# Two 64-byte buffers move in front of the three large tiles of a one-core decode kernel

## The chip, the core and the metric

The kernel runs on one core of a Trainium2 chip. Its time is the time on the device in microseconds (us), as the runs give it. The profile adds one profiled execution, with the start and duration of each instruction on TensorE (PE, with weight loads apart as PEld), VectorE (DVE), ScalarE (ACT), GpSimd (POOL) and SyncE (SP), and with the transfers between the chip's memory and the core's on-chip memory (SBUF). SBUF has 128 partitions; a buffer takes the same byte range in each of them, so that one byte address per buffer says where it lies.

## The reference

One decode step of a transformer block, batch B = 2, one new token each, model width D = 512, in bf16:

- q = layernorm(x) @ wq, in 32 heads of Dh = 128. For each of the 2 x 32 heads, with its own cache of Sk = 8192 keys and values: scores = q . k / sqrt(128), p = softmax(scores), o = p @ v. The heads' outputs side by side, times wo, are added to x and give h.
- gate = layernorm(h) @ W_gate, up = layernorm(h) @ W_up (512 to 1376), gate times (gate > 0), times up, times W_down (1376 to 512), added to h.

The two caches have 2 x 32 x 8192 x 128 bf16 values each, 134 MB per cache. All of it is read once, so the kernel moves some 281 MB into SBUF. There is one multiplication and one addition per cached value, since every head has a single query.

## The kernel before

**Tiles.** A "quad" is four heads of one batch row. Its keys are 8 MB: one tile of 128 partitions x 32768 bf16, 65,536 bytes per partition (`TILE`, L54). The three buffers `bufs[0..2]` of that size (`tile0`, `tile1`, `tile2`, made in L90 from the pool `big`) hold all that streams in. There are 16 quads; the first 15 are whole steps (`steps[0..14]`, `LASTQ` is 14), and the last quad is worked as two pairs of heads (`steps[15]`, `steps[16]`) whose keys and values come in pieces of 4 MB or 1 MB. The step's key tile and value tile go round the three buffers (L137, L138: buffers 2i mod 3 and 2i+1 mod 3). wq lies in the first half of `tile2` before the first steps; at the end wo, W_gate, W_up and W_down take freed halves of the three tiles (L121 to L127).

**A transfer.** `load_tile` (L160) issues a transfer on SyncE's queue: each partition's row is one contiguous run of 65,536 bytes in memory and one in SBUF. The rows of W_gate and W_up (L613 to L616) are 5,504 bytes, those of W_down and of the last wo pieces 1,024 to 8,192.

**A step.** For step i: PE transposes 24 or 32 of the tile's 256 key columns and multiplies them with q (`scores_pe`, L329, with copies by ACT, L353); DVE multiplies all other keys by the q of their head (`products`, L378, in place, with `qrep`) and adds the products up by halving four times and a reduction (`scores`, L396, L398); DVE and ACT make the maximum and the exponentials (`largest_of_own`, L411; L418 writes the sums of the exponentials into `zs`); DVE lays them out as weights (`place_own`, L423, into `pgq`); PE multiplies the weights with the value tile in 64 matrix products (`values`, L449). Every fourth step or so the group of heads is normalised (`close`, L318, where `own_sums`, L299, reads `zs`).

**Order.** The order on each engine is written out by hand (`tc.manual_schedule`, L187); nothing reorders it. The value tile of step i+1 is loaded into the buffer of step i's keys as soon as DVE has reduced them (L528, SyncE waits for L398); the key tile of step i+2 goes into the buffer of step i's values when PE has used them (L552, SyncE waits for L449). So two transfers are under way or queued while one step is computed. Both wait on SyncE's queue, in this order.

**Where things lie.** Pools are laid out in the order in which they are made (L80 to L83), and buffers in the order of their lines, each rounded up to 32 bytes. A reserved block fills the bytes up to 16,384, four constants take 128 bytes, and then `front` begins: `qTs` (L87) and `ocol` (L88), 128 bytes each. The tiles follow. In the built program `tile0` begins at byte 16,768 of each partition, `tile1` at 82,304 and `tile2` at 147,840, each 384 bytes behind a multiple of 512, and 128 behind a multiple of 256. Behind the tiles stand the pool `consts` (`qrep` and all below it, among them `zs`, 64 bytes, L99, and `qzp`, 64 bytes, L103) and the pool `small`. `qzp` holds the queries of the last two heads' pairs, and PE loads it as weights in the last two steps (L342).

Of the kernel before, what the change touches and what calls it, by code (L numbers as in the profile page):

```python
# [23 lines left out]
def kernel(  # L24
# [14 lines left out]
    P = nc.NUM_PARTITIONS  # L39
    B, Sq, D = A_x.shape  # L40
# [6 lines left out]
    bf16 = mybir.dt.bfloat16  # L47
    f32 = mybir.dt.float32
# [3 lines left out]
    NQ = Hq // NH  # L52
# [27 lines left out]
    front = ctx.enter_context(tc.tile_pool(name="front", bufs=1))  # L80
    big = ctx.enter_context(tc.tile_pool(name="big", bufs=1))
    consts = ctx.enter_context(tc.tile_pool(name="consts", bufs=1))
# [3 lines left out]

    qTs = front.tile([P, B, Hq], bf16)  # L87
    ocol = front.tile([P, Hq, B], bf16)  # L88

    bufs = [big.tile([P, TILE], bf16, name=f"tile{k}") for k in range(3)]  # L90

# [4 lines left out]
    pv = consts.tile([P, VG * Dh], f32)  # L96
    pick = consts.tile([P, VG, 4, NH], f32)
    zc = consts.tile([P, B, NQ, NH], f32)
    zs = consts.tile([P, B, NQ], f32)  # L99
    own = consts.tile([P, NH], f32)  # L100
    ownb = consts.tile([P, NH, VG], bf16)
    ecol = consts.tile([P, TILE // Dh], bf16)
    qzp = consts.tile([P, 2, 16], bf16)  # L103
    qz = consts.tile([P, 2 * QZ], bf16)
    ident = consts.tile([P, P], bf16)
    ident_f = consts.tile([QZ, QZ], f32)
# [647 lines left out]
```

## Time and profile before

| | us |
|---|---|
| median of 3 runs | 662.56 (661.42 to 663.75) |
| the profiled execution's own time | 661.14 |
| its span, from the first to the last instruction | 659.3 |
| DVE busy | 557.4 (85%) |
| PE busy (matmuls) | 353.1 (54%) |
| ACT busy | 122.9 (19%) |
| transfers: share of the span in which the 16 DMA engines carry packets of SyncE's queue | 99.0% |

The page gives the DMA engines' share as a mean over 16 engines. A packet is a contiguous run that one of them moves; the packets under 512 bytes are almost all the 4-byte notes that tell a semaphore of a transfer's end. In the answers by stretch ("DMA share, GB/s"), a packet's bytes and time can fall into the neighbouring stretch, so that a share can stand a little above 1.00; the quotient of the two columns is the rate of a busy DMA engine, times 16. "issue to landing" is the time from the instruction that starts a transfer until its semaphore says that it has ended, waiting in the queue included. PEclk is the granted TensorE clock as a share of full speed; its mean is 0.759 here.

### The profile page before, as it was taken

The page shows a single profiled execution, that of the slowest core. Times are in us where ns is not written, and L with a number is a line of the kernel's source. Part 1 is how long each engine was busy: PE and PEld are TensorE (multiplying, and loading weights), DVE is VectorE, ACT ScalarE, POOL GpSimd, SP SyncE. Part 2 cuts the span into 40 slices and gives each one's busy share as a digit, 9 for nine tenths or more (in the row PEclk, how much of TensorE's full clock was granted, in tenths as well). Part 3 has the DMA queues.
Part 4 walks back from the last instruction along what each step waited for, and adds up shares of the span by engine and source line. Part 5 has one row for each costly group of instructions (what it writes and reads, how often), then busy time and mean ns, then how long its engine had stood idle before and what let it go on. Part 6 is the DMA issues. An engine that isn't in the chain of part 4 may idle for free.

```text
span 659.3 us, 5118 instructions
## 1 busy us (share of the span) xinstructions
PE 353.1 (54%) x2123; PEld 160.8 (24%) x2123; DVE 557.4 (85%) x248; ACT 122.9 (19%) x335; POOL 7.6 (1%) x35
## 2 busy tenths in 40 slices
PE   3540924709174480917438092562909358291987
PEld 1220311304022130402214041220403224030456
DVE  2399697989979699997979979896997969999981
ACT  1130030301103020020302102030210304201870
POOL 3000000000000000000000000000000000000010
PEclk9865875959778595977859687695968869686985
DMA  9999999999999999999999999999999999999997
GB/s 382 445 442 445 433 399 441 441 446 434 414 433 430 441 438 421 433 437 426 441 425 434 437 426 433 421 442 437 425 434 427 437 438 425 437 430 412 426 414 279
DMA packets 7946, 281.40 MB, mean 427 GB/s; under 512 B 882, under 2 KB 1780, under 8 KB 2804
## 3 DMA queue, kind: packets, MB, share of 16 engines
q1 hardware_dynamic: 7920, 281.09, 99.0%
q8 instruction: 16, 0.26, 0.2%
q14 instruction: 6, 0.05, 0.0%
q10 hardware_dynamic: 4, 0.00, 0.0%
HBM read 281.09 MB, written 0.00 MB: 426 GB/s over the span
## 4 chain that ended last, share of the span: by engine, by line
DVE 47%; DMA 34%; PE 17%; ACT 1%; issue 1%; SPq 0%; DVEq 0%; ACTq 0%
DMA tile<-in_A_k_cache_dram 28%; DVE tile L378 21%; DVE tile L396 20%; PE pv_ps L449 16%; DMA tile<-in_A_v_cache_dram 3%; DVE scol L398 3%; DMA tile<-in_B_W_up_dram 2%; DVE pgq L423 1%; DMA tile<-in_B_W_down_dram 1%; ACT ecol L418 1%; DVE pm L402 1%; DVE qrep L398 0%; DVE pm L413 0%; DVE hmax L415 0%; PE z_ps L308 0%
## 5 line engine op out<-in xcount | busy, mean ns | idle before, releaser
L449 PE MATMUL pv_ps<-tile,pgq 128*16 128x512 bf16 x960 | 241.8, 417 | 236.4 <-DVE pgq L423 225.0
L378 DVE TENSOR_TENSOR tile<-tile,qrep 128x29696 bf16<-128x29696 bf16 (+3 forms) x16 | 232.4, 14522 | 37.7 <-DMA tile<-in_A_k_cache_dram 37.7
L396 DVE TENSOR_TENSOR tile<-tile 128x14848 bf16<-128x14848 bf16 (+7 forms) x68 | 236.5, 3477 | 2.3
L449 PEld LDWEIGHTS <-pgq 128*16 128x16 bf16 x960 | 91.0, 97 | 376.4 <-DVE pgq L423 235.1
L353 ACT ACTIVATE tile<-t_ps 128x1024 bf16<-128x1024 bf16 x53 | 52.5, 1022 | 18.6 <-PE t_ps L352 18.2
L454 ACT ACTIVATE pv<-pv_ps 16x512 f32<-16x512 f32 (+1 forms) x16 | 9.4, 589 | 234.0 <-PE pv_ps L449 233.9
L418 ACT ACTIVATE ecol<-scol,nmax 128x256 bf16<-128x256 f32 x14 | 7.1, 508 | 196.7 <-DVE nmax L417 196.7
L352 PE MATMUL t_ps<-ident,tile 128*128 128x128 bf16 x424 | 32.7, 230 | 18.1 <-DMA tile<-in_A_k_cache_dram 18.1
L343 PE MATMUL row_ps<-tile,qz 128*24 128x512 bf16 (+1 forms) x98 | 31.0, 399 | 18.6 <-ACT tile L353 18.5
L352 PEld LDWEIGHTS <-tile 128*128 128x128 bf16 x424 | 26.1, 103 | 33.3 <-DMA tile<-in_A_k_cache_dram 18.7
L398 DVE TENSOR_REDUCE scol<-tile 128x232 f32<-128x1856 bf16 (+1 forms) x14 | 28.9, 2067 | 0.5
L423 DVE TENSOR_TENSOR pgq<-ecol,ownb 128x1024 bf16<-128x1024 bf16 x15 | 10.4, 692 | 10.3 <-ACT ecol L418 10.3
L384 ACT ACTIVATE tile<-tile 128x128 bf16<-128x128 bf16 x60 | 17.6, 295 | 1.9 <-DVE tile L378 1.9
L378 DVE TENSOR_TENSOR tile<-tile,qpair 128x4096 bf16<-128x4096 bf16 (+3 forms) x4 | 15.5, 3882 | 0.0
L343 PEld LDWEIGHTS <-qz 128*24 128x24 bf16 (+1 forms) x98 | 7.9, 93 | 28.7 <-issue 23.5
L249 PE MATMUL q_ps<-tile,xn 128*2 128x512 bf16 x32 | 9.7, 469 | 8.4 <-DMA tile<-in_A_wq_dram 8.4
L252 DVE CAST tile<-q_ps 2x512 bf16<-2x512 f32 x8 | 5.4, 678 | 10.2 <-PE q_ps L249 10.2
L370 ACT ACTIVATE scol<-sc_ps 32x24 f32<-32x24 f32 (+1 forms) x56 | 11.7, 209 | 7.7 <-PE sc_ps L365 7.2
L365 PE MATMUL sc_ps<-ident_f,tile 24*128 24x24 f32 (+2 forms) x68 | 7.2, 220 | 11.0 <-ACT tile L361 11.0
L361 ACT ACTIVATE tile<-row_ps 24x512 f32<-24x512 f32 (+2 forms) x17 | 10.0, 586 | 13.4 <-PE row_ps L343 13.4
L312 DVE RECIPROCAL rz<-z_ps 128x16 f32<-128x16 f32 (+1 forms) x4 | 0.9, 236 | 13.1 <-PE z_ps L308 13.1
L384 ACT ACTIVATION_READ_ACCUMULATOR tile<-tile 128x1 f32 x60 | 11.3, 188 | 0.0
(130 smaller groups left out, 132.9 us busy)
## 6 DMA issues: line engine op xcount, KB each, us to landing
tile<-in_A_k_cache_dram SPq DMA_DIRECT2D x2, 4096.0 KB, 22.8
tile<-in_A_wq_dram SPq DMA_DIRECT2D x1, 4096.0 KB, 12.1
tile<-in_A_v_cache_dram SPq DMA_DIRECT2D x1, 4096.0 KB, 19.7
tile<-in_A_v_cache_dram SPq DMA_DIRECT2D x4, 1024.0 KB, 21.0
tile<-in_A_wo_dram SPq DMA_DIRECT2D x1, 2048.0 KB, 24.2
tile<-in_B_W_gate_dram SPq DMA_DIRECT2D x2, 688.0 KB, 13.8
tile<-in_B_W_up_dram SPq DMA_DIRECT2D x2, 688.0 KB, 12.9
tile<-in_A_wo_dram SPq DMA_DIRECT2D x1, 1024.0 KB
```

The source lines that it names most:

```text
L343: nc.tensor.matmul(out=row_ps, lhsT=z, rhs=s.kt[:, (nv + c0 + k) * Dh:(nv + c0 + k + 4) * Dh], start=(u == 0), stop=(u == U - 1),)
L352: nc.tensor.transpose(t_ps[:, k, :], s.kt[:, t * Dh:(t + 1) * Dh], ident)
L353: nc.scalar.activation(out=s.kt[:, (nv + c0) * Dh:(nv + c0 + TPC) * Dh], in_=t_ps.rearrange("p t s -> p (t s)"), func=ACT.Copy,)
L361: nc.scalar.activation(out=rows, in_=row_ps, func=ACT.Copy)
L370: nc.scalar.activation(out=scols[s.i][r, nv:s.nt].rearrange("p (u t) -> p t u", t=4), in_=sc_ps[r, :, :, j], func=ACT.Copy,)
L378: nc.vector.tensor_tensor(out=kv, in0=kv, in1=_free(s.qr, 0, [[0, n], [1, Dh]]), op=ALU.mult)
L384: nc.scalar.activation(out=kv, in_=kv, func=ACT.Copy, accum_out=scols[s.i][:, t:t + 1])
L396: nc.vector.tensor_tensor(out=lo, in0=lo, in1=hi, op=ALU.add)
L398: nc.vector.tensor_reduce(out=scol[:, s.na:s.nv], in_=_free(s.kt, s.na * Dh, [[Dh, s.nv - s.na], [1, 8]]), axis=AXIS.X, op=ALU.add,)
L418: nc.scalar.activation(out=ecol, in_=scols[s.i], func=ACT.Exp, scale=SCALE, bias=nmax, accum_out=zs[:, s.b, s.g:s.g + 1],)
L423: nc.vector.tensor_tensor(out=s.pg, in0=_free(ecol, 0, [[VG, s.nt // VG], [0, NH], [1, VG]]), in1=_free(ownb, 0, [[0, s.nt // VG], [VG, NH ...
L449: nc.tensor.matmul(out=pv_ps[s.i][r, :], lhsT=s.pg[:, u].rearrange("p j t -> p (j t)"), rhs=s.vt[:, u * VG * Dh:(u + 1) * VG * Dh], start= ...
```

## The change

`zs` and `qzp` are made in the pool `front`, behind `qTs` and `ocol`, and no longer in `consts`. They take 64 bytes each, so all that follows begins 128 bytes later, until the places where they stood: `tile0` at 16,896, `tile1` at 82,432, `tile2` at 147,968, all multiples of 512; `qrep` to `zc` are 128 bytes further on as well, `own`, `ownb` and `ecol` 64 bytes, and from `qz` on every buffer keeps its address. No instruction is added, taken away or moved in its engine's order, no size and no transfer's source changes.

```diff
     qTs = front.tile([P, B, Hq], bf16)
     ocol = front.tile([P, Hq, B], bf16)
+    zs = front.tile([P, B, NQ], f32)
+    qzp = front.tile([P, 2, 16], bf16)
 
     bufs = [big.tile([P, TILE], bf16, name=f"tile{k}") for k in range(3)]
 ...
     zc = consts.tile([P, B, NQ, NH], f32)
-    zs = consts.tile([P, B, NQ], f32)
     own = consts.tile([P, NH], f32)
     ownb = consts.tile([P, NH, VG], bf16)
     ecol = consts.tile([P, TILE // Dh], bf16)
-    qzp = consts.tile([P, 2, 16], bf16)
     qz = consts.tile([P, 2 * QZ], bf16)
```

## The prediction

> **What bounds the kernel now.** I read the transfers first: the head of the DMA view, its queues, and what the transfers take from issue to landing.
>
> ```profile
> span 659.3 us, 5118 instructions
> DMA packets 7946, 281.40 MB, mean 427 GB/s; under 512 B 882, under 2 KB 1780, under 8 KB 2804
> q1 hardware_dynamic: 7920, 281.09, 99.0%
> ...
> tile<-in_B_W_gate_dram SPq DMA_DIRECT2D x2, 688.0 KB, 13.8
> ...
> DMA to landing us min/median/max: 19.7/25.6/51.4
> ```
>
> SyncE's queue carries 281.09 MB in 7920 packets, and its packets fill 99.0% of the time of the 16 DMA engines. Nothing that only shortens a wait on another engine can gain more than the missing 1.0%. The last line is the answer for line 165, the line that loads key and value tiles. Now the rate by stretches, in columns of busy time per engine, then the granted clock, the share of the DMA engines and their GB/s:
>
> ```profile
> 4.00:66.00 62.00, 20.13 (x112) 9.15 (x112) 40.75 (x31) 10.70 (x22) 2.41 (x18) 0.72 1.02 440
> 66.00:144.00 78.00, 40.62 (x196) 16.77 (x196) 67.94 (x18) 10.98 (x23) 0.00 (x0) 0.72 0.99 430
> 144.00:221.00 77.00, 39.82 (x204) 17.30 (x204) 68.61 (x23) 11.54 (x24) 0.00 (x0) 0.77 1.00 434
> 221.00:299.00 78.00, 39.56 (x198) 16.73 (x198) 69.94 (x26) 11.49 (x24) 0.00 (x0) 0.76 1.00 431
> 299.00:376.00 77.00, 40.34 (x204) 17.40 (x204) 68.66 (x22) 11.53 (x24) 0.00 (x0) 0.77 1.00 433
> 376.00:454.00 78.00, 40.03 (x198) 16.84 (x198) 69.70 (x26) 11.50 (x24) 0.00 (x0) 0.76 1.01 433
> 454.00:532.00 78.00, 42.75 (x224) 18.72 (x224) 67.27 (x24) 13.69 (x26) 0.00 (x0) 0.78 1.00 433
> ```
>
> From 4 to 532 us the DMA engines are never short of work (0.99 to 1.02), and GB/s by share is 429 to 434 in every stretch: a busy set of 16 engines moves about 433 GB/s, 27.1 GB/s each. At that rate 281.09 MB take 649.2 us; the other 10.1 us of the span are the start, the small packets and the end. The chain of waits calls only a third of itself DMA, because it names whichever engine released the next step:
>
> ```profile
> DVE 47%; DMA 34%; PE 17%; ACT 1%; issue 1%; SPq 0%; DVEq 0%; ACTq 0%
> ...
> DVE tile L378 <- DMA tile<-in_A_k_cache_dram: 37.7, 11, 5.6
> ```
>
> The second row, from the view of waits, shows that DVE arrives early: 11 times its products wait for a key tile, 3.4 us on average. And a tile of 8.39 MB takes 19.4 us at 433 GB/s while the median landing is 25.6 us, so the usual tile transfer stands some 6 us in the queue. DVE and PE can each lose a few us per step, or gain any amount, before the transfers notice.
>
> **The change part by part.** (1) The moved buffers themselves. `zs` and `qzp` keep their sizes and their users.
>
> ```profile
> L299 DVE TENSOR_TENSOR zc<-zs,own x4: 161/168/168, 224.0 to 610.5; 128x16 f32<-128x16 f32 x3, 128x12 f32<-128x12 f32 x1
> ...
> L343 PEld LDWEIGHTS <-qzp x8: 82/86/87, 615.0 to 625.1; 128*8 128x8 bf16 x8
> ```
>
> These rows are their minimum, median and maximum in ns. Four reads of 168 ns and eight loads of 86 ns: even doubled they would cost 0.7 + 0.7 us, and all but the last few lie under running transfers. I take nothing. If the cover were gone, 1.4 us is the end of it.
>
> (2) The engines' accesses to the tiles. The large operands are DVE's and PE's:
>
> ```profile
> L378 DVE TENSOR_TENSOR tile<-tile,qrep 128x29696 bf16<-128x29696 bf16 x10 | 156.2, 15623 | 24.5 <-DMA tile<-in_A_k_cache_dram 24.5
> L396 DVE TENSOR_TENSOR tile<-tile 128x14848 bf16<-128x14848 bf16 x11 | 86.8, 7892 | 0.4
> L449 PE MATMUL pv_ps<-tile,pgq 128*16 128x512 bf16 x960 | 241.8, 417 | 236.4 <-DVE pgq L423 225.0
> ```
>
> 29,696 elements in 15,623 ns and 14,848 in 7,892 ns are the same 1.9 elements per ns and a small constant, for operands that start half a head apart and for `qrep` behind the tiles. The tiles, `qrep` and `pgq` all move by the same 128 bytes, so their places relative to each other stay. The nearest rows therefore give no gain and no loss; a gain would be hidden behind the transfers, and a loss is hidden up to the 3.4 us that DVE waits per step, 10% of the 34 to 35 us that it is busy per step (67.94 to 69.94 us in stretches of two steps). I take nothing.
>
> (3) The transfers' destinations: the only part on the path. Each row now starts 0 instead of 384 bytes behind a multiple of 512. What such a start costs is not in the trace as a row, since nearly all rows of before start in the same way. Bounds: of the 7920 packets, 882 are under 512 B (the notes of completion); the other 7038 are 440 per DMA engine. What each costs beyond its bytes shows where they are short. Rows of 688 KB / 128 partitions, 5,504 bytes, are nearly all that moves here:
>
> ```profile
> 643.50:649.50 6.00, 5.28 (x153) 5.13 (x153) 1.08 (x7) 0.00 (x0) 0.00 (x0) 0.50 1.03 413
> 649.50:655.50 6.00, 5.63 (x108) 5.22 (x106) 1.08 (x7) 0.59 (x1) 0.00 (x0) 0.50 0.83 311
> 655.50:659.30 3.80, 1.19 (x30) 0.83 (x27) 0.38 (x2) 0.00 (x0) 0.00 (x0) 0.50 0.01 2
> ```
>
> At 413 GB/s such a packet takes 5,504 x 16 / 413 = 213 ns; at 433 it would take 203 ns. So whatever a packet costs at its start and end, offset included, is about 10 ns. If all of it were due to the offset, the change would save 440 x 10 ns = 4.4 us; if none is, nothing. A loss has its own bound under the rivals. The rows reject one thing: if the start had to be filled up from the multiple of 512 below, 384 bytes at 27.1 GB/s would be 14 ns, more than the whole 10. Filled up from the multiple of 256 below, it is 128 bytes, 4.7 ns, and 440 x 4.7 = 2.1 us. Between 0 and 4.4 us the row nearest to the bulk of the bytes is that of the long rows, where 10 ns stand against 2,420 ns (65,536 bytes at 27.1 GB/s): the offset is not seen in their rate at all. I take 1.0 us saved, the middle of what is left below the filled-up start, and keep 0 and 4.4 us for the range.
>
> The Trainium skill speaks to this in "DMA: Bandwidth & Descriptors", section "How a descriptor splits into AXI transactions": a transaction begins at a multiple of 256 B, and a descriptor that begins elsewhere fetches the bytes before it for nothing, in beats of 32 B. Its examples are about reading the source, and here it is the destination that is off by 128 B, four beats; read for both sides it gives the 2.1 us above, read as written it gives nothing, and no run so far tells which. The same page, section "Where 436 GB/s comes from", puts a ceiling of 435.2 GB/s on the way into SBUF. The 433 GB/s of the stretches agree with it within 0.5%, and by it even a perfect rate saves no more than 281.09 / 433 - 281.09 / 435.2, some 3.3 us; that speaks against expecting much.
>
> What is saved passes on to the end. It adds up packet by packet, per transfer it is far under the 6 us that one queues, and the final work behind the last packets (655.5 to 659.3 us, 2 GB/s in the last row) keeps its length. The sum against the profiled execution: 661.14 us (span 659.3 and 1.8 around it) - 1.0 = 660.1. The runs' median is 1.4 us above that execution, so the same saving gives 662.56 - 1.0 = 661.6 us. A measurement of this kernel can tell about 0.3%, or 2.0 us, from no change: its three runs span 2.3 us.
>
> **The rivals.** (a) The start of a row has a real price. Each packet then loses at least the filled-up 128 bytes: 2.1 to 4.4 us, 658.2 to 660.5 us. For it: some 10 ns per packet exist and must be made of something, and the transfers are so full that each ns comes through. Against it: the constant may belong to the packet itself and stay.
>
> (b) The change puts the transfers into a worse place: rows that begin on a multiple of 512 meet the engines' accesses, or each other, in the same piece of SBUF. The place is the steady part, where DVE and PE read tiles while DMA writes another. The transfers' rate would drop; from 433 to 429 GB/s, the lowest quotient of the stretches above, costs 655.2 - 649.2 = 6.0 us, 668.6 us. It decides from a drop of 1.3 GB/s on, 2.0 us. Against it: all tiles move together, so their distances stay, and the rate does not follow the engines' work:
>
> ```profile
> 200.00:220.00 20.00, 5.55 (x47) 3.21 (x44) 19.83 (x6) 5.17 (x10) 0.00 (x0) 0.72 1.00 430
> 220.00:240.00 20.00, 15.84 (x62) 6.23 (x63) 14.90 (x10) 0.60 (x2) 0.00 (x0) 0.76 1.03 446
> ```
>
> 430 GB/s at share 1.00 with DVE busy all the time and PE for a quarter, 433 per full share with PE three times as busy. For it: the trace of before holds one offset only, so it cannot show what another one does.
>
> (c) The change doesn't do what it says. That can be left out: the built program has the tiles at 16,896, 82,432 and 147,968, multiples of 512, and the same instructions.
>
> (d) The rate itself rises, since each piece of a long row, not only its first, is cut differently. From 433 to 440 GB/s, the highest row, would save 10.4 us: 652.2 us. Against it: that row has share 1.02, its quotient is 431; nothing above 434 is ever sustained.
>
> **How the numbers follow.** My forecast, a saving of 0 to 2.0 us, has a chance of 0.40. Rival (a) has 0.32 and (d) 0.04; together they make faster by over 0.3%: 0.36. Rival (b) has 0.24, the chance of slower. Within 0.3% is 0.40. The range reaches from the end of (a), 662.56 - 4.4 = 658.2, to the price of (b), 668.6; outside lie (d), 0.04, and the part of (b) that costs more, 0.10. As cases of both signs hold much of the chance, the likeliest one's own range is 660.5 to 662.6.
>
> **What would show it.** Right: the stretch from 4 to 532 us keeps 429 to 434 GB/s per full share, the queue keeps 99% and 7920 packets, and DVE's 15,623 and 7,892 ns and PE's 417 ns (at the same clock) stay. Rival (a): the stretch of the 5,504-byte rows goes from 413 towards 423 GB/s, and all else ends 2 us earlier. Rival (b): a lower rate at a full share, with DVE's wait for key tiles growing from 37.7 us; or, if the engines pay instead of the transfers, longer L378 and L396, a wait of DVE near zero and a DMA share below 0.99. The prediction is wrong if the long rows' rate moves by over 1.3 GB/s either way.

## The result and the profile after

The changed kernel takes 660.34 us (median of 13 runs, 659.58 to 662.12) against 662.56 us before (13 runs, 661.28 to 663.75): 2.2 us less, ratio 0.9968, 95% interval 0.9959 to 0.9976. A second comparison, under the experiments, gave 0.9982 (0.9973 to 0.9991), 1.2 us. The sign is certain; the size is not, it lies between 0.1% and 0.4%.

The profiled execution of the changed kernel took 660.24 us, 0.9 us less than that of before. First the head of its DMA view and the landings of line 165, then its stretches with the same columns as in the prediction:

```profile
span 658.5 us, 5118 instructions
DMA packets 7946, 281.40 MB, mean 427 GB/s; under 512 B 882, under 2 KB 1780, under 8 KB 2804
q1 hardware_dynamic: 7920, 281.09, 99.0%
...
DMA to landing us min/median/max: 19.4/25.5/51.7
```

```profile
4.00:66.00 62.00, 19.72 (x112) 8.92 (x112) 40.92 (x32) 10.47 (x21) 2.42 (x18) 0.76 1.02 442
66.00:144.00 78.00, 38.28 (x196) 16.25 (x196) 67.75 (x18) 11.22 (x24) 0.00 (x0) 0.76 0.99 430
144.00:221.00 77.00, 40.87 (x204) 17.54 (x204) 68.69 (x23) 11.53 (x24) 0.00 (x0) 0.74 1.00 433
221.00:299.00 78.00, 39.32 (x198) 16.55 (x198) 70.07 (x27) 11.50 (x24) 0.00 (x0) 0.76 1.00 433
299.00:376.00 77.00, 39.94 (x204) 17.29 (x204) 68.84 (x22) 11.54 (x24) 0.00 (x0) 0.77 1.00 432
376.00:454.00 78.00, 39.76 (x198) 16.77 (x198) 70.03 (x27) 11.50 (x24) 0.00 (x0) 0.76 1.01 436
454.00:532.00 78.00, 42.78 (x224) 18.70 (x224) 67.11 (x24) 13.70 (x26) 0.00 (x0) 0.76 1.00 431
```

The same packets fill the same 99.0% of a slightly shorter span, and the stretches still give 431 to 434 GB/s per full share. A difference of 0.2% does not show there. It shows a little where the rows are short; the engines' groups of instructions and DVE's wait for key tiles have hardly moved:

```profile
643.50:649.50 6.00, 5.29 (x162) 5.13 (x160) 0.96 (x7) 0.00 (x0) 0.00 (x0) 0.50 1.02 417
649.50:655.50 6.00, 5.75 (x115) 5.38 (x112) 1.08 (x7) 0.59 (x1) 0.00 (x0) 0.50 0.64 241
...
L449 PE MATMUL pv_ps<-tile,pgq 128*16 128x512 bf16 x960 | 240.7, 416 | 240.8 <-DVE pgq L423 227.8 <-DMA tile<-in_A_v_cache_dram 13.1
L378 DVE TENSOR_TENSOR tile<-tile,qrep 128x29696 bf16<-128x29696 bf16 x10 | 156.2, 15623 | 24.1 <-DMA tile<-in_A_k_cache_dram 24.1
L396 DVE TENSOR_TENSOR tile<-tile 128x14848 bf16<-128x14848 bf16 x11 | 86.8, 7892 | 0.4
...
DVE tile L378 <- DMA tile<-in_A_k_cache_dram: 36.9, 11, 5.6
```

413 became 417 GB/s, and the transfers are through earlier in the next stretch (311 GB/s before, 241 now, as less is left to move). DVE's 15,623 and 7,892 ns are the same to the nanosecond, PE's 417 ns became 416, and DVE's wait went from 37.7 to 36.9 us.

The trace also holds the time of each single packet. Here they are counted by duration for three lengths of a row: 65,536 bytes (the loads of whole tiles), 8,192 (one piece of wo and four of values) and 5,504 (W_gate and W_up). "Shortest usual" is the shortest duration that more than a few packets have:

```
kernel   bytes   count   shortest usual   usual+1..+20 ns   longer   mean up to +20   mean of all
before    5504     512   211 ns: 79%          15%            6.1%      211.6 ns        214.3 ns
changed   5504     512   211 ns: 99%           1%            0.4%      211.0 ns        212.0 ns
before    8192     640   309 ns: 29%          70%            0.3%      313.4 ns        314.7 ns
changed   8192     640   309 ns: 100%          0%            0.2%      309.0 ns        309.4 ns
before   65536    3840   2418 ns: 45%         54%            1.2%     2420.5 ns       2424.9 ns
changed  65536    3840   2418 ns: 92%          5%            2.4%     2418.3 ns       2422.1 ns
```

The shortest packets of before already took what nearly all take now. The change did not make the fast packet faster; it took away a delay, of 1 to 13 ns in nearly all cases, that other packets had. Summed over SyncE's queue and divided by 16, packet times went from 653.045 to 651.903 us, 1.14 us less. That is one execution of each, and no firm size: in the traces of the experiments the sum is 652.33 to 653.60 us in three with tiles at 0 or 256 behind a multiple of 512, and 653.12 and 653.80 in two with tiles at 128 and 448.

### The profile page after: what moved, and what is told of

The parts are those of the page before. It is cut to its first block, busy times and chain, and to the rows that moved or that the text cites. A ratio compares the mean times of both kernels' runs of the same rounds, so it can differ in the third digit from the quotient of the medians.

```text
span 658.5 us, 5118 instructions
## 1 busy us (share of the span) xinstructions
PE 349.5 (53%) x2123; PEld 159.0 (24%) x2123; DVE 557.5 (85%) x248; ACT 123.1 (19%) x335; POOL 7.0 (1%) x35
## 4 chain that ended last, share of the span: by engine, by line
DVE 52%; DMA 29%; PE 18%; issue 1%; ACT 1%; SPq 0%; DVEq 0%; ACTq 0%
DMA tile<-in_A_k_cache_dram 29%; DVE tile L378 23%; DVE tile L396 22%; PE pv_ps L449 15%; DVE scol L398 3%; DVE pgq L423 1%; ACT ecol L418 1%; DVE pm L402 1%; DVE qrep L398 1%; PE o_ps L472 1%; DVE pm L413 0%; PE z_ps L308 0%; PE att_ps L505 0%; PE d_ps L701 0%; DVE hmax L415 0%
## 5 line engine op out<-in xcount | busy, mean ns | idle before, releaser
L378 DVE TENSOR_TENSOR tile<-tile,qrep 128x29696 bf16<-128x29696 bf16 (+3 forms) x16 | 232.4, 14522 | 36.9 <-DMA tile<-in_A_k_cache_dram 36.9
L343 PE MATMUL row_ps<-tile,qz 128*24 128x512 bf16 (+1 forms) x98 | 29.6, 383 | 18.9 <-ACT tile L353 18.9
```

The lines of the kernel that those rows point to most:

```text
L343: nc.tensor.matmul(out=row_ps, lhsT=z, rhs=s.kt[:, (nv + c0 + k) * Dh:(nv + c0 + k + 4) * Dh], start=(u == 0), stop=(u == U - 1),)
L378: nc.vector.tensor_tensor(out=kv, in0=kv, in1=_free(s.qr, 0, [[0, n], [1, Dh]]), op=ALU.mult)
```

## The experiments

Theory A: a row whose destination does not begin at some multiple pays a price per row, in the transfers. Theory B: the new place of `zs` and `qzp` matters. Theory C: the price goes by bytes or time, not by rows. Theory D: the distance between the starts of source and destination counts. And apart from these: does the price need the engines' work beside the transfers?

### Which multiple, and is it the two buffers

Each edit is made to the kernel before; the comments are added here.

```diff
-    ident_f = consts.tile([QZ, QZ], f32)
+    ident_f = front.tile([QZ, QZ], f32)       # tiles at 0 behind a multiple of 512; zs, qzp as before
```

> Tiles at a multiple of 512 again, but by another buffer: ident_f (128 bytes) stands in front, zs and qzp stay in consts. Theory A (the destination's start decides): the same as the change, about 2.2 us less than before, 660.3 us. Theory B (the new place of zs and qzp decides): no change against before, 662.5 us.

```diff
-    ocol = front.tile([P, Hq, B], bf16)
+    ocol = consts.tile([P, Hq, B], bf16)      # tiles at 256 behind a multiple of 512
```

> ocol goes from front into consts, so the tiles begin 256 bytes behind a multiple of 512. If a multiple of 256 is enough: 2.1 to 2.2 us less than before, 660.3 us. If only a multiple of 512 counts: as before, 662.5 us. If a start is filled up from the multiple of 512 below, something between: a third of the gain is left out, 661.1 us would be it.

```diff
-    qTs = front.tile([P, B, Hq], bf16)
-    ocol = front.tile([P, Hq, B], bf16)
+    qTs = consts.tile([P, B, Hq], bf16)
+    ocol = consts.tile([P, Hq, B], bf16)      # front empty, tiles at 128
```

> qTs and ocol go into consts, front is empty, the tiles begin 128 bytes behind a multiple of 512. Filled up from the multiple of 256 below, a row's start costs the same 128 bytes as before: 662.5 us, no change. If the distance from the multiple of 512 counts, it is 128 bytes instead of 384, and two thirds of the gain come: about 661 us. If any multiple of 128 will do, before would have nothing to lose and the change could not have gained, so this one is excluded already.

```diff
-    zs = consts.tile([P, B, NQ], f32)
+    zs = front.tile([P, B, NQ], f32)          # tiles at 448
```

> Only zs goes in front: the tiles begin 448 bytes behind a multiple of 512, 192 behind a multiple of 256, 64 behind a multiple of 128. Filled up from the multiple of 256 below: 192 bytes, 7.1 ns per packet instead of 4.7, about 1.0 us more than before, 663.6 us. If a row off its multiple costs one constant piece of time, the same as before, 662.5 us. If what counts is a collision between DMA engines and no filling, again as before, or worse by an amount that no bytes explain.

The changed kernel itself was run again later, beside the loads-alone kernels below:

> The changed kernel once more, on the chip of the next three and against the kernel before there. If the two moved buffers have no part in it, the saving is that of ident_f in front and of the tiles at 256, some 1.1 us (0.17%), within their intervals, so that the 2.2 us of the first comparison were at the upper edge. If zs and qzp in front bring the other half, 2.2 us (0.32%) again.

Medians of 11 to 13 runs; the kernel before has its own median in each set (662.56, 661.80 and 662.00 us). The last column is the mean duration of the 8,192-byte packets, without the 0.3% or fewer that are over 20 ns late:

```
tiles begin at   kernel                      us       ratio to before (95%)         8192-byte rows
0                the change                  660.34   0.9968 (0.9959 to 0.9976)     309.0 ns
0                the change, again           660.81   0.9982 (0.9973 to 0.9991)     309.0 ns
0                ident_f in front            660.78   0.9983 (0.9974 to 0.9992)     309.0 ns
256              ocol in consts              660.59   0.9984 (0.9975 to 0.9993)     309.0 ns
128              qTs and ocol in consts      662.06   1.0000 (0.9989 to 1.0010)     313.4 ns
384              before                                                             313.4 ns
448              zs in front                 662.20   1.0009 (0.9998 to 1.0019)     313.7 ns
```

Theory B falls: other buffers in front do what `zs` and `qzp` do, as well as the changed kernel did when it was run again. A multiple of 256 is enough; 512 has no part in it. The times alone, with intervals of 0.2%, could not tell a part of the gain from all of it, but the packets do: 309.0 ns at 256 as at 0. And 128, 384 and 448 behind a multiple of 512 (128, 128 and 192 behind one of 256) cost the same within the intervals. These would still have room for the 1.0 us that 192 bytes filled up would take on top of 128; it is again the packets that speak against it, with 4.7 ns at 192 bytes instead of 4.4, not 7.1. So it is no filling up of bytes at the rate of a transfer.

The first comparison and the second, of the same kernel, differ: 2.2 against 1.2 us. Their intervals touch between 0.9973 and 0.9976. Three comparisons stand near 0.998; why the first is larger stays open.

### Rows or bytes

```diff
         n = s.nt * Dh
+        pieces = 8 if s.quad else pieces
         w = n // pieces
```

Put into the kernel before (tiles at 384) and into the changed one (tiles at 0):

> The kernel before with each 8 MB tile loaded in 8 transfers with rows of 8,192 bytes instead of 65,536: 8 times as many packets in the 30 large loads, 26,880 more, 1,680 more per DMA engine. At some 10 ns per packet and its share of completion notes (240 transfers x 9 ns or so) both kernels of this pair get slower by 16 to 20 us. Theory A (a price per row's start): the gap between this one and its pair grows with the packets, from 2.2 us to 2.2 + 1,680 x 4.7 ns = 10 us. Theory C (the price goes by bytes, or by time): the gap stays near 2.2 us.

> The same cut into rows of 8,192 bytes in the changed kernel, tiles at multiples of 512. Theory A: 10 us less than its pair at 384. Theory C: 2.2 us less.

677.20 us (4 runs, 677.01 to 677.31) and 668.72 us (4 runs, 668.62 to 668.97). The gap is 8.5 us instead of 1.2 to 2.2: it grows with the rows, so theory C falls. The pair has 38,160 packets in SyncE's queue, 31,360 of them of 8,192 bytes: 1,960 per DMA engine. 8.5 us / 1,960 is 4.3 ns per row, and the packets themselves say 313.5 against 309.0 ns. The expected 10 us had 4.7 ns in it and 2.2 us at the start; both were a little high. Two stretches of each, first at 384, then at 0, with the rate that a busy set of DMA engines gives:

```profile
span 675.5 us, 5482 instructions
q1 hardware_dynamic: 38160, 281.10, 100.0%
...
221.00:299.00 78.00, 39.37 (x198) 16.53 (x198) 67.85 (x26) 11.49 (x24) 0.00 (x0) 0.76 1.01 422
299.00:376.00 77.00, 40.67 (x204) 17.48 (x204) 66.56 (x22) 11.52 (x24) 0.00 (x0) 0.74 1.01 421
```

```profile
span 667.0 us, 5482 instructions
q1 hardware_dynamic: 38160, 281.10, 99.9%
...
221.00:299.00 78.00, 40.31 (x198) 16.87 (x198) 69.08 (x25) 11.49 (x24) 0.00 (x0) 0.76 1.01 427
299.00:376.00 77.00, 39.90 (x204) 17.29 (x204) 67.51 (x23) 11.52 (x24) 0.00 (x0) 0.77 1.01 427
```

Here, where every 8,192 bytes pay, the price is 1.3% of the rate and can be read from the stretches: 421 or 422 against 427 GB/s at the same share. Both kernels are slower than with long rows, by 15.4 us (at 384, 661.84 us before in that set) and some 8 us (at 0, against 660.34 to 660.81 in other sets); 16 to 20 us had been expected for both. The second is what eight times the rows and transfers cost without the offset; how it divides between a row's packet, the notes and the rest was not measured.

### The transfers alone

The kernel is cut down to the 30 loads of whole tiles, round the three buffers, and a store of a few rows; a buffer of 256 or 384 bytes in front sets where the tiles begin:

```diff
-    (all computation and all other transfers)
+    lead = front.tile([P, 256 // 2], bf16)              # or 384 // 2: tiles at 384, or at 0
+    for i in range(30):
+        cache = A_v_cache if i % 2 else A_k_cache
+        b, g = divmod(i // 2, NQ)
+        for k in range(TILE // ROW):                    # ROW: 65,536 or 8,192 bytes
+            nc.sync.dma_start(
+                out=bufs[i % 3][:, k * ROW:(k + 1) * ROW],
+                in_=_dram(cache, (b * Hkv + NH * g) * Sk * Dh + SRC + k * ROW, [[TILE, P], [1, ROW]]),
+            )
```

With rows of 65,536 bytes:

> Nothing is computed: the 30 whole tiles of keys and values alone are loaded into the three buffers, one behind the other, 251.7 MB, tiles 384 bytes behind a multiple of 512. At 433 GB/s: 581 us and some 5 us of start and end. If the gain needs the engines' accesses beside the transfers, this one and its pair at 0 are equal, and their packets too. If it is between the transfers alone, this one is slower by 240 packets per DMA engine x the price: 1.1 us at 4.7 ns.

> The same loads alone with the tiles at multiples of 512 (the 30 tiles are loaded, nothing is computed). Transfers alone: 1.1 us less than its pair at 384, and packets of 65,536 bytes nearly all of one duration. Engines needed: equal.

587.85 us at 384 and 587.42 us at 0 (2 runs each): 0.4 us, less than the 1.1 expected and too little to decide. The packets show why it is small: up to 20 ns late the means are 2421.1 and 2418.3 ns, which times 240 would be 0.7 us. But 3.5% of the packets at 0 are later than that, against 0.4% at 384, and with them the means turn round (2423.4 and 2424.0 ns), so that the packets do not give the 0.4 us either. So the pair was too weak, and short rows were tried, `SRC` being 0, 384 and 384 bytes for the three:

> The 30 loads alone, nothing computed, in rows of 8,192 bytes, tiles at 384 behind a multiple of 512, sources at multiples of 8,192. If the price lies between the transfers alone, the rows cost the 4 to 4.5 ns each that they cost beside the engines' work: some 604 us, against 595.5 us for rows without it (587.4 us of the long rows plus the 8.1 us by which the cut into 8,192 bytes slowed the changed kernel). If the engines' accesses are needed: 595.5 us.

> As the run before it, but the source of each row begins 384 bytes further on too, so that source and destination are both off by the same 384 bytes (other values are loaded, nothing is computed). Theory A (the destination's own start counts): as the run before it, about 604 us. Theory D (the distance between the starts of source and destination counts): 595.5 us.

> The same loads with the tiles at multiples of 512 and the sources 384 bytes off (nothing is computed). Theory A: 595.5 us, since the destination is straight. Theory D: about 604 us, as the first of the three. If any offset on either side costs the same, all three stand at about 604 us.

```
destination   source    us (2 runs)   8192-byte rows
off           straight  603.43        313.5 ns
off           off       603.45        313.5 ns
straight      off       595.48        309.0 ns
```

One stretch of each, in this order; no engine computes, so that the columns are GpSimd, the clock, the share and GB/s:

```profile
20.00:300.00 280.00, 0.00 (x0) 1.00 1.01 422
```

```profile
20.00:300.00 280.00, 0.00 (x0) 1.00 1.01 422
```

```profile
20.00:300.00 280.00, 0.00 (x0) 1.00 1.01 427
```

The rates are those of the pair with all its computation, so the engines have no part in it. 603.43 - 595.48 = 7.95 us over 1,920 rows per DMA engine is 4.1 ns per row. For these rows the destination alone decides: theory D falls with the second run, and with the third a source 384 bytes off costs nothing that can be seen. Source and destination both straight were not run here; the 309.0 ns of such rows in the kernel with its computation, and the 595.5 us that had been expected without a price, stand in for it.

## Why the prediction was right or wrong

**What bounds the kernel: right.** Only the transfers could give, and they gave less than 1%. The engines' instructions kept their times, and the DMA engines kept their 99.0%.

**Part 1, the moved buffers, nothing: shown.** `ident_f` in their stead gives the same saving as the repeated run (0.9983 and 0.9982).

**Part 2, the engines' accesses, nothing: shown** by the group rows (15,623 and 7,892 ns in both), and by the loads alone, which have the same price without any engine.

**Part 3, the transfers' destinations: right in place and sign, the term was a little small.** 1.0 us was taken; 2.2 and 1.2 us were measured, the packets of the profiled pair sum to 1.14. The bounds, 0 and 4.4 us, hold. By the first comparison rival (a), with 2.1 us or more, had it; by the repetition my forecast did. That the size came near is luck: 1.0 us was the middle between two bounds, not the reading of a price. That a row's start has a real price is what rival (a) said, and there it was right. What failed is the step "the row nearest to the bulk of the bytes is that of the long rows [...]: the offset is not seen in their rate at all". It is true that it can't be seen in the stretches, which differ by 1% among themselves in either kernel, but the packets' durations in the same trace, 45% of them at 2418 ns and 54% a few ns later, would have shown that something made the rows of before uneven.

**How a start pays: the filled-up 128 bytes were wrong, though their 4.7 ns came close.** Rows of 8,192 bytes pay 4.1 to 4.5 ns on average (by the two pairs' times and by their packets), but 27 to 30% of them pay nothing (7% at 192 bytes), 192 bytes cost 4.7 ns and not 7.1, and the shortest time is the same with and without the offset. Rows of 65,536 bytes pay 2.2 ns beside the engines' work and 2.8 without. The "about 10 ns" mostly stay with any row: 309 ns without the offset are still 7 ns more than 8,192 bytes take at 27.1 GB/s (302 ns), and the rows of 5,504 bytes, from which the 10 ns were read, went from 214.3 to 212.0 ns, against 203 ns. What delays the rows is not settled: the runs show when, not how.

**A row's own start is not the whole rule.** The prediction read the 5,504-byte rows as rows with the offset, but half of them are straight in either kernel: each transfer of W_gate and W_up begins 5,504 bytes behind the one before it (L613 to L616), which is 21.5 times 256. So in the changed kernel half of them still begin 128 bytes behind a multiple of 256, and yet 507 of the 512 take 211 ns; in the kernel before, again with one half straight, only 402 do. All rows that the experiments cut are whole multiples of 256 bytes long: off the multiple, such a row touches one more stretch of 256 bytes than it would otherwise (33 instead of 32 for 8,192 bytes), while a row of 5,504 touches 22 either way. That would fit the changed kernel, but not by itself the delays of before. There, source and destination of each of these rows lie differently by 128 bytes to the multiples of 256, and in the changed kernel alike; that is theory D, which fell for rows of 8,192 bytes. No run tried these rows by themselves, so this stays open.

The Trainium skill's rule in "DMA: Bandwidth & Descriptors", "How a descriptor splits into AXI transactions", speaks of a start that is off a multiple of 256 B. Its 256 is the multiple that the runs show, 512 is not. But the side is the other one: the rule is worded for reading, and here an off source cost nothing that can be seen (595.48 us, 309.0 ns per row), an off destination 4.1 ns per row. The ceiling of 435.2 GB/s that the Trainium skill states in "DMA: Bandwidth & Descriptors", "Where 436 GB/s comes from", was not passed: 429 to 434 GB/s before and 431 to 434 after, per full share.

**Rivals (b) and (d): not seen.** Per full share the stretches give 429 to 434 GB/s before and 431 to 434 after; no change of 1.3 GB/s stands out from that spread. The stretch of short rows went from 413 to 417 GB/s, part of the way to the 423 of rival (a), which is about the rate with 4.7 ns less per row.

**The pass to the end: right.** The landings' median moved from 25.6 to 25.5 us, still 6 us over a transfer of its own, DVE's wait for key tiles from 37.7 to 36.9, and nothing new became late.

## What to carry to other kernels

Where transfers fill the DMA engines all the time and rows are whole multiples of 256 bytes, let each partition's destination begin at a multiple of 256; 128 bytes of small buffers in front did that here for nothing. What it is worth can be estimated beforehand: rows per DMA engine times 2 to 4.5 ns. Here that was about 0.2% with the bulk of the bytes in rows of 65,536, and 1.3% in rows of 8,192. Cutting rows short cost as much again even with straight starts (some 8 us here), so the length of a row comes first. And the durations of single packets show such a price where rates by stretch do not.

## What was unexpected

The offset's price is not the same for each row: some rows pay nothing and others up to 13 ns or a little more, for equal lengths and equal offsets. And straight long rows may be late more often: 2.4 to 4.2% of the 65,536-byte packets were over 20 ns late in the four traces of the whole kernel with tiles at 0 or 256, against 1.2 to 3.3% at 128, 384 and 448, and in the loads alone 3.5% against 0.4%. The ranges overlap, and it is one trace of each kernel. It gives back part of the saving with long rows (the means of all packets fall by 2.8 ns at best, 2424.9 to 2422.1, and in one trace rise, to 2428.9) and not with rows of 8,192 bytes, where 0.1% are late either way in the runs cut into them. Its cause was not tried.
